# The taps' first transform stage with whole 128-row matmuls instead of row halves

## The chip, the core and the metric

The kernel runs on one core of a Trainium2 chip. The metric is the device time of one execution in microseconds, the median over runs. One profiled execution of the kernel before is at hand, with its trace. Engines: TensorE (PE for matmuls, PEld for weight loads), VectorE (DVE), ScalarE (ACT), GpSimd (POOL), and SyncE (SP), whose queue issues the DMA transfers.

## What is computed

Two mixers over the same 2048 tokens of 576 channels are blended by a gate. A long convolution (S4) makes 2048 taps per channel from 128 complex modes and convolves by FFT; a layer of product-key experts (PEER) scores 64 x 64 experts for 32 heads, keeps two per head, and weighs rows of two tables of 4096 x 576.

```
x = A_u                                             # [1, 2048, 576]
g = sigmoid((x * gate_w).sum(-1))
K[d, l] = Re sum_n C[d, n] dB[d, n] exp(dt A[d, n] l)   # the taps
a = irfft(rfft(x, 4096) * rfft(K, 4096))[:2048] + x * Dskip
q = x @ w_q;  s1 = q1 @ k1.T;  s2 = q2 @ k2.T           # 32 heads, 64 keys each
top 2 of s1 and of s2 -> 4 candidates -> top 2 -> softmax g_k, expert e_k
b = sum over heads and k of g_k * gelu(x . u[e_k]) * v[e_k]
out = g * a + (1 - g) * b
```

## The kernel before

Matrix products run in split fp16: each operand is a high and a low half, and three of the four cross products are summed. Two families of *groups* make the bulk of TensorE's work. An `s` group scores 128 tokens against the folded weights of four heads (`whl`, `wrem`); an `a` group multiplies 512 tokens with 128 experts (`uhl`, `wrem`). Each sums 13.5 rows of 128 contractions over 512 columns in one PSUM bank: 4 blocks of 128 channels times 3 cross products, and a rest of 64 channels.

A group is written by `start_group` in one of two ways. `halved` cuts every matmul into an upper part (rows 0 to 63) and a lower part (rows 64 to 127), 27 matmuls of 64 rows; `rows` puts the upper ones on a queue `upper` and, when those are through, the lower ones on a list `lower`, and `row_slot` emits one upper matmul of one group beside one lower matmul of the group ahead of it. The two use different rows of the array and different banks. `triple` writes the group as 14 matmuls of 128 rows one after another (the rest as two passes with one operand stored twice). The kernel before has `triple` in its code, but its condition `caps["sc"] < 4` never holds once the loop runs, so all groups but the first four are halved.

The program's order is fixed when it is built. Generators are resumed by `pump` against a planned clock; each carries one strand of work: `k_gen` makes the taps, `k_stage1` and `products` transform them, `scores_top` finds the two best of each head, `act_post` stores the activations, `w_half` folds the next weights (`wn` small sums, `wb` the fold), `gating` forms the gates, `v_norm` reads the gate's inputs and the second table (`vn`, `vj`). `quota` sets how many of the eight PSUM banks groups (`sc`) and strands (`wb`) may hold. `chained[0]` says that the halves are in use; `total` and `k_factors` then put their small sums on the same queue.

The change is in the taps' transform. When all 36 chunks of taps are stored in DRAM (`k_store`), `freq` is spawned, which loads them back in another layout (`ksb`, four loads, with the tables `tk`) and runs `k_stage1`: 32 steps `w`, each with two outputs of 288 columns (`k1_w_0`, `k1_w_1`), each a sum of two 128-row products. `k1o` copies them from two banks to one of four buffers, and `sk_d` stores it. `products` follows: it loads spectra of the input and of the taps (`ui`, `ki`), finishes both transforms (`pr`, `pi`), multiplies and transforms back (`pv`). Groups run in between all the while. When they have all run, the experts' values are gathered with one-hot matmuls (`S`) and summed (`o`).

SP issues transfers in program order; an issue that waits holds up all behind it. `vn` loads have two buffers, `k1o` four.

Of the kernel before, what the change touches and what calls it, by code (L numbers as in the profile page):

```python
# [140 lines left out]
def body(ctx: ExitStack, tc: tile.TileContext, xT, au, par, logdt, dskip, gatew, wq, kT, uT, vv,  # L141
# [5 lines left out]
    clock = [0.0]  # L147
# [11 lines left out]
    def key(x):  # L159
        n = x.tensor.name  # L160
        return (n, x.offset) if n in columns else n

    def size(x):
        n = 1
        for d in x.shape[1:]:
            n *= d
        return n
# [41 lines left out]
    def mm(o, l, r, start, stop, cost=None):  # L209
        m = l.shape[0] > 64, 128 if size(l) > 64 else size(l)  # L210
        if m != tiling[0]:
            tiling[0] = m
            clock[0] += 0.13 if m == (True, 128) else 0.1
        clock[0] += (size(r) * (4 if r.dtype == F32 else 1) / 2400 + 0.003) if cost is None else cost
        rdy[key(o)] = clock[0] + 0.4
        return T.matmul(o, l, r, start=start, stop=stop)  # L216
# [4 lines left out]
    def rows(up, low, then=None, first=False):  # L221

        g = {"up": deque(up), "low": deque(low), "then": then, "done": False, "end": None, "short": first}
        (upper.appendleft if first else upper.append)(g)
        return g
# [28 lines left out]
                    g["then"]()  # L254

    chained = [False]

    def total(p, cols):

# [45 lines left out]
    slots, caps, owed = {}, {}, {}  # L305
# [6 lines left out]
    def quota(**kw):  # L312
        for tag, n in kw.items():
            if tag in banksets:
                caps[tag] = n
                continue
            lst = slots.setdefault(tag, [])
            d = n - caps.get(tag, 0) - owed.get(tag, 0)
            caps[tag], owed[tag] = n, 0
            while d > 0:  # L320
                lst.append(clock[0])
                d -= 1
            while d < 0 and lst:
                lst.remove(min(lst))
                d += 1
            owed[tag] = -d if d < 0 else 0
# [13 lines left out]
    def take(tag, name):  # L340
        lst = slots[tag]
        assert lst, name
        lst.remove(min(lst))
# [66 lines left out]
    sc = cp.tile([128, 192], F32, name="sc")  # L410
# [601 lines left out]
    def k_store(c, kb):  # L1012
        yield from ready(kb)
        yield from need("ko")
        take("ko", "ko")
        ko = kg.tile([128, 2, 2 * NI * R2], F16, name="ko", tag="ko", bufs=1)
        kq = kb.rearrange("p (c i q) -> p q c i", c=2, i=NI)
        kz = ko.rearrange("p z (q c i) -> p z q c i", c=2, i=NI)
        S.activation(kz[:, 0], kq, AF.Copy)
        yield from ready(ko)  # L1020
        V.tensor_sub(kz[:, 1], kq, kz[:, 0])
        free("kb", ko, of=kb)
        yield from ready(ko)
        kstored[0] += 2
        dma(k_d[c].rearrange("p z m q -> p z (m q)"), ko)
        free("ko", k_d)
        if kstored[0] == NCK:
            while uf != 0:
                yield 0.3
            KG.__exit__(None, None, None)  # L1030
            quota(sc=5, wb=4, kb=0, raw=2)
            spawn(freq())


# [231 lines left out]
    def k_stage1(ksb, fk, tabs):  # L1266
        enter, leave, count = ring(3)

        def tail(w, o, pbs, gs):
            while not all(g["done"] for g in gs):  # L1270
                yield 0.2
            yield from ready(*pbs)
            for hh in range(2):
                copy(o[:, 288 * hh:288 * hh + 288], pbs[hh][:, :288])
                free("wb", o, of=pbs[hh])
            yield from ready(o)
            dma(pair_rows(sk_d, w), o)
            leave(w)

        for w in range(32):  # L1280
            tkt = tabs[w // 16]
            yield from ready(tkt, ksb)
            yield from enter()
            o = fk.tile([128, D], F32, tag="s1o", name=f"k1o{w}", bufs=4)
            pbs, gs = [], []
            yield from need("wb", 2)
            for hh in range(2):
                pb = bank("wb", f"k1_{w}_{hh}")
                pbs.append(pb)
                gs.append(rows(*([(pb[:, :288], tkt[h:h + 64, w % 16, n],  # L1290
                                   ksb[h:h + 64, 2 * hh:2 * hh + 2, :, w, :].rearrange("p j c i -> p (j c) i"),
                                   h == 0 and n == 0, h == 64 and n == 1) for n in range(2)] for h in (0, 64)), first=True))
            spawn(tail(w, o, pbs, gs))
            del pb, pbs
        while count() < 32:
            yield 0.5
# [102 lines left out]
    def freq():  # L1399
        nonlocal ff, ab, iota_a, iota_b  # L1400
        ff = FG.__enter__()
        wrems.append(ff.tile([128, 2, 512], F16, name="wrem3"))
        ksb = KS.__enter__().tile([128, 4, NCK // 2, 32, 2 * NI], F16, name="ksb")
        fk = FK.__enter__()
        tabs = [fk.tile([128, 16, 2, 128], F16, tag="tk", name=f"tk{w0}", bufs=2) for w0 in (0, 16)]
        for w0, tkt in zip((0, 16), tabs):
            dma(tkt, tk_d[:, w0:w0 + 16, :])
        for j in range(4):
            while wire[0] > clock[0] + 2:
                yield 0.3  # L1410
            dma(ksb[:, j].rearrange("p c w i -> p c (w i)"),
                k_d[:, 32 * j:32 * j + 32].rearrange("c l z m n -> (l z m) c n"))
        spawn(v_norm(), 4)
        spawn(gating(0), 20)
        yield from k_stage1(ksb, fk, tabs)
        FK.__exit__(None, None, None)
        KS.__exit__(None, None, None)
        v_pool(0, 3)
        spawn(v_work())
        fp = FP.__enter__()  # L1420
        quota(sc=4, wb=5)
        yield 3
        yield from products(fp)
        FP.__exit__(None, None, None)
        quota(sc=4, wb=4)
        ab = ctx.enter_context(tc.tile_pool(name="ab", bufs=1, side="right"))
        iota_a = ab.tile([128, 128, 2], F16, name="iota_a")
        iota_b = ab.tile([128, 64, 2], F16, name="iota_b")
        V.tensor_copy(iota_a, cst[:, 384:512, None].to_broadcast([128, 128, 2]))
        V.tensor_copy(iota_b, cst[:, 512:576, None].to_broadcast([128, 64, 2]))  # L1430
        spawn(prep(0))
        v_pool(3, 5)
        while not gated or not gates:
            yield 0.5
        FG.__exit__(None, None, None)
        WJ.__exit__(None, None, None)
        v_pool(5, 8)
        shut.append(1)
# [444 lines left out]
    def start_group(g):  # L1883

        x = xb[tb_of(g)]
        if len(g) == 2:
            c, t = g
            pb = bank("sc", f"s{c}_{t}")
            args = (pb, *whl[c], x), (slice(128 * (t % 4), 128 * (t % 4) + 128), slice(0, 512), True)

            def then():
                spawn(scores_top(c, t, pb))
                used(("w", c), ("x", t // 4))
        else:
            c, tb, j = g
            if c == 7 and not got:
                got.append(1)
                V.tensor_reduce(out=nut[:, 0:1], in_=nu, axis=AX, op=OP.max)
                V.scalar_tensor_tensor(nut[:, 1:2], nut[:, 0:1], 1100.0, nx2, op0=OP.mult, op1=OP.mult)
                got.append(root_scale(nut[:, 1:2], 1.0))  # L1900
                V.tensor_scalar(s_wg, got[1][0], 2.0 ** -14, None, op0=OP.mult)
            if c in i_u and (c, tb) not in scales:
                scales.add((c, tb))
                V.tensor_scalar(i_a[:, c, tb:tb + 1], i_x[:, tb:tb + 1], i_u[c], None, op0=OP.mult)
            pb = bank("sc", f"a{c}_{tb}_{j}")
            args = (pb, *uhl[c], x), (slice(0, 512), slice(128 * j, 128 * j + 128), False)

            def then():
                spawn(act_post(c, tb, j, pb))
                used(("u", c), ("x", tb))  # L1910
        parity[0] = tb_of(g) % 2
        if caps["sc"] < 4:
            while upper or lower:
                row_slot()
            chained[0] = False
            triple(*args[0], *args[1])
            then()
            return
        chained[0] = True
        rows(*halved(*args[0], tb_of(g), *args[1]), then)  # L1920
        while len(lower) > 2 and sum(len(x["low"]) for x in lower[:-1]) > 6:
            row_slot()
            if not upper:
                return
# [111 lines left out]
```

## Time and profile before

| | |
|---|---|
| median of 3 runs | 1452.56 us (1451.73 to 1454.49) |
| the profiled execution | 1451.91 us |
| its span | 1450.1 us |
| granted TensorE clock, mean | 0.999 |
| DMA | 215.89 MB, mean 149 GB/s |
| first and last product of the taps' stage | 685.0 to 732.2 us |
| `sk_d` stores | 32 of 288 KB |

Busy shares and the chain of waits come from the page of the profile; times from a stretch come from the stages (busy time of each engine, matmul count in brackets, then clock, DMA share, GB/s) and from the order of time, where a row is: start, length, engine, line, operation, output and inputs, shape, count, and in square brackets the idle time ahead of it and what ended it. All matmuls carry line 216 and all work of the other engines line 136, since helpers record them; so one goes by the tiles' names.

### The profile page before, as it was taken

What the parts mean: (1) busy time and instruction counts of PE and PEld (TensorE: products, weight loads), DVE (VectorE), ACT (ScalarE), POOL (GpSimd) and SP (SyncE); (2) the same over time, 40 slices, a digit from 0 to 9 for tenths busy, and PEclk for the clock granted to TensorE, in tenths of its full rate; (3) what the DMA queues carried; (4) which work ended last, traced back from release to release, by engine and by line L of the source; (5) the groups of instructions that cost most, each with busy time, mean ns of one, the idle gap of its engine ahead of it and who ended that gap; (6) DMA issues with size and microseconds to landing.
All of it is one profiled execution on the core that took longest, in us unless ns stands there. A gap on an engine that the chain in (4) does not pass through costs nothing.

```text
span 1450.1 us, 44027 instructions
## 1 busy us (share of the span) xinstructions
PE 1422.8 (98%) x17654; PEld 902.6 (62%) x17654; DVE 1193.5 (82%) x4597; ACT 830.3 (57%) x1444; POOL 477.1 (33%) x488
## 2 busy tenths in 40 slices
PE   7999999999999999999999999999999999999998
PEld 3465566554565665455664444446887887888787
DVE  5887699889889988777789998699999988888860
ACT  6547887987888887664656665564333223323310
POOL 0443265552571663530557899400000000000000
PEclk9999999999999999999999999999999999999999
DMA  9333543343351331238785788687442433342400
GB/s 315 116 111 100 167 134 110 99 128 110 110 157 47 120 104 46 78 125 269 253 275 173 255 273 310 218 254 223 155 153 86 135 121 106 122 146 68 157 9 17
DMA packets 134381, 215.89 MB, mean 149 GB/s; under 512 B 10913, under 2 KB 79905, under 8 KB 127777
## 3 DMA queue, kind: packets, MB, share of 16 engines
q1 hardware_dynamic: 134080, 213.01, 45.5%
q8 instruction: 138, 2.26, 0.6%
q14 instruction: 67, 0.54, 0.1%
q10 hardware_dynamic: 96, 0.07, 0.0%
HBM read 141.74 MB, written 71.30 MB: 147 GB/s over the span
## 4 chain that ended last, share of the span: by engine, by line
PE 86%; DMA 5%; DVE 4%; issue 1%; SPq 1%; ACT 1%; POOL 1%; ACTq 0%; POOLq 0%; DVEq 0%
PE a L216 25%; PE o L216 24%; PE s L216 21%; PE S L216 4%; PE kb L216 2%; PE pr L216 2%; PE wb L216 2%; DMA wq<-in_wq_dram 1%; SPq L207 1%; PE kP L216 1%; PE y L216 1%; DVE i L136 1%; PE pv L216 1%; DVE m L136 1%; PE u L216 1%
## 5 line engine op out<-in xcount | busy, mean ns | idle before, releaser
L216 PE MATMUL s<-whl,xb 64*128 64x512 f16 x3072 | 468.8, 377 | 0.5 <-ACT k1o L136 0.3
L216 PE MATMUL a<-xb,uhl 64*128 64x512 f16 (+1 forms) x3024 | 455.5, 376 | 0.3 <-DVE go L136 0.2
L216 PE MATMUL o<-vhl,wh 128*128 128x288 f16 x3072 | 387.1, 286 | 0.0
L216 PEld LDWEIGHTS <-wh 128*128 128x128 f16 x3072 | 295.9, 98 | 76.2 <-issue 3.7
L216 PEld LDWEIGHTS <-xb 64*128 64x128 f16 x3456 | 226.8, 94 | 167.5 <-issue 15.2
L216 PEld LDWEIGHTS <-uhl 64*128 64x128 f16 (+1 forms) x3024 | 195.8, 94 | 165.1 <-issue 6.9
L136 ACT ACTIVATE wh<-gl,s_wg 128x1024 f16<-128x1024 f32 x64 | 68.7, 1137 | 197.4 <-DVE gl L136 197.4
L136 POOL TENSOR_TENSOR CS<-CS,ex 128x512 f32<-128x512 f32 x72 | 90.6, 1290 | 167.2 <-DVE ex L136 167.2
L216 PE MATMUL s<-wrem,xb 64*128 64x512 f16 x384 | 122.2, 376 | 0.0
L216 PE MATMUL a<-xb,wrem 64*128 64x512 f16 (+1 forms) x380 | 120.2, 376 | 0.0
L136 ACT ACTIVATE go<-a,i_a 128x512 f32<-128x512 f32 x98 | 66.9, 684 | 85.6 <-PE a L216 57.0
L136 DVE FIND_INDEX8 i<-m,s 128x8 uint32<-128x64 f32 x520 | 104.7, 219 | 0.0
L136 DVE TENSOR_TENSOR gl<-S,gl 128x256 f32<-128x256 f32 x256 | 90.3, 414 | 15.6 <-PE S L216 6.1
L136 POOL TENSOR_TENSOR e<-aN,rt 128x512 f32<-128x512 f32 x72 | 83.9, 1185 | 46.6 <-PE kb L216 46.5
L136 DVE FIND_INDEX8 i<-m,sx 128x8 uint32<-128x64 f32 x504 | 99.2, 216 | 0.0
L136 DVE MAX8 m<-s 128x8 f32<-128x64 f32 x520 | 74.1, 212 | 26.8 <-PE s L216 22.7
L136 DVE SCALAR_TENSOR_TENSOR wh<-gl,s_wg,wh 128x1024 f16<-128x1024 f32 x64 | 79.7, 1278 | 10.4 <-ACT wh L136 10.4
L136 ACT ACTIVATE gl<-gl 128x1024 f32<-128x1024 f32 x64 | 63.4, 1045 | 40.5 <-DMA gl<-g_d 40.5
L136 DVE TENSOR_TENSOR Bg<-Be,vals 128x1024 f16<-128x1024 f16 x128 | 82.7, 688 | 2.2
L136 ACT ACTIVATE CS<-CS 128x1024 f32<-128x1024 f32 x72 | 74.6, 1049 | 6.4 <-DVE CS L136 6.1
L136 DVE TENSOR_TENSOR A<-iota_a,vals 128x2048 f16<-128x2048 f16 x64 | 77.7, 1214 | 0.0
L216 PEld LDWEIGHTS <-A 128*128 128x128 f16 x2048 | 70.1, 97 | 6.4 <-issue 2.8
(206 smaller groups left out, 2356.4 us busy)
## 6 DMA issues: line engine op xcount, KB each, us to landing
g_d<-go SPq DMA_DIRECT2D x128, 256.0 KB, 2.7
gl<-g_d SPq DMA_DIRECT2D x32, 1024.0 KB, 5.6
wq<-in_wq_dram SPq DMA_DIRECT2D x16, 1152.0 KB, 5.9
su_d<-us SPq DMA_DIRECT2D x32, 288.0 KB, 2.6
sk_d<-k1o SPq DMA_DIRECT2D x32, 288.0 KB, 2.8
ui<-su_d SPq DMA_DIRECT2D x16, 576.0 KB, 4.3
ki<-sk_d SPq DMA_DIRECT2D x16, 576.0 KB, 5.6
vn<-in_vv_dram SPq DMA_DIRECT2D x32, 288.0 KB, 4.5
```

The costliest lines, as they stand in the source:

```text
L136: return f(*a, **k)
L207: (q or DQ).dma_start(o, i)
L216: return T.matmul(o, l, r, start=start, stop=stop)
```

## The change

While `k_stage1` is planned (from the storing of the last taps until `products` begins), groups are written by `triple`, after the halves that are still open have been emitted alone, and `chained[0]` is cleared. `k_stage1` then writes its products as two matmuls of 128 rows for each output. The groups' share of banks in the stage is four instead of five. With `phase[0]` at `"products"` groups are halved again. The other values of `phase` decide nothing, and `clock[0] < 0` is never true.

```diff
--- before.py
+++ after.py
@@ -254,6 +254,7 @@
                     g["then"]()
 
     chained = [False]
+    phase = ["taps"]
 
     def total(p, cols):
 
@@ -1028,7 +1029,8 @@
             while uf != 0:
                 yield 0.3
             KG.__exit__(None, None, None)
-            quota(sc=5, wb=4, kb=0, raw=2)
+            quota(sc=4, wb=4, kb=0, raw=2)
+            phase[0] = "k1"
             spawn(freq())
 
 
@@ -1287,6 +1289,11 @@
             for hh in range(2):
                 pb = bank("wb", f"k1_{w}_{hh}")
                 pbs.append(pb)
+                if not chained[0]:
+                    for n in range(2):
+                        mm(pb[:, :288], tkt[:, w % 16, n], ksb[:, 2 * hh:2 * hh + 2, :, w, :].rearrange("p j c i -> p (j c) i"),
+                           n == 0, n == 1)
+                    continue
                 gs.append(rows(*([(pb[:, :288], tkt[h:h + 64, w % 16, n],
                                    ksb[h:h + 64, 2 * hh:2 * hh + 2, :, w, :].rearrange("p j c i -> p (j c) i"),
                                    h == 0 and n == 0, h == 64 and n == 1) for n in range(2)] for h in (0, 64)), first=True))
@@ -1419,10 +1426,12 @@
         spawn(v_work())
         fp = FP.__enter__()
         quota(sc=4, wb=5)
+        phase[0] = "products"
         yield 3
         yield from products(fp)
         FP.__exit__(None, None, None)
         quota(sc=4, wb=4)
+        phase[0] = "last"
         ab = ctx.enter_context(tc.tile_pool(name="ab", bufs=1, side="right"))
         iota_a = ab.tile([128, 128, 2], F16, name="iota_a")
         iota_b = ab.tile([128, 64, 2], F16, name="iota_b")
@@ -1909,7 +1918,7 @@
                 spawn(act_post(c, tb, j, pb))
                 used(("u", c), ("x", tb))
         parity[0] = tb_of(g) % 2
-        if caps["sc"] < 4:
+        if clock[0] < 0 or phase[0] in ("k1",):
             while upper or lower:
                 row_slot()
             chained[0] = False
```

The names in the rows below carry the step and then a number of the buffer. On TensorE at the entry, where `freq` has just been spawned, two `a` groups are open. Before:

```order
L216 LDWEIGHTS uhl6_9266
L216 MATMUL a6_0_1_11060<-xb0_145,uhl6_9266 128x512
L216 LDWEIGHTS xb0_145
L216 MATMUL s5_0_11209<-whl5_10645,xb0_145 128x512
L216 LDWEIGHTS uhl6_9266
L216 MATMUL a6_0_1_11060<-xb0_145,uhl6_9266 128x512
L216 LDWEIGHTS xb0_145
L216 MATMUL s5_0_11209<-whl5_10645,xb0_145 128x512
```

Now:

```order
L216 LDWEIGHTS uhl6_9266
L216 MATMUL a6_0_1_11060<-xb0_145,uhl6_9266 128x512
L216 LDWEIGHTS uhl6_9266
L216 MATMUL a6_0_1_11060<-xb0_145,uhl6_9266 128x512
L216 LDWEIGHTS uhl6_9266
L216 MATMUL a6_0_1_11060<-xb0_145,uhl6_9266 128x512
L216 LDWEIGHTS wrem0_114
L216 MATMUL a6_0_1_11060<-xb0_145,wrem0_114 128x512
L216 LDWEIGHTS uhl6_9266
L216 MATMUL a6_1_0_11092<-xb1_146,uhl6_9266 128x512
```

The lower halves stood beside the upper halves of `s5_0`; now all 18 of them stand alone, and `s5_0` follows them in 128 rows. On TensorE at the first product of the taps' stage, before:

```order
L216 MATMUL s5_7_11590<-whl5_10645,xb1_146 128x512
L216 LDWEIGHTS tk0_11205
L216 MATMUL k1_0_1_11717<-ksb_11201,tk0_11205 128x288
L216 LDWEIGHTS xb1_146
L216 MATMUL s5_7_11590<-whl5_10645,xb1_146 128x512
L216 LDWEIGHTS tk0_11205
L216 MATMUL k1_0_1_11717<-ksb_11201,tk0_11205 128x288
L216 LDWEIGHTS xb1_146
L216 MATMUL s5_7_11590<-whl5_10645,xb1_146 128x512
```

Now:

```order
L216 LDWEIGHTS xb1_146
L216 MATMUL s5_7_11585<-whl5_10645,xb1_146 128x512
L216 LDWEIGHTS tk0_11205
L216 MATMUL k1_0_0_11596<-ksb_11201,tk0_11205 128x288
L216 LDWEIGHTS tk0_11205
L216 MATMUL k1_0_0_11596<-ksb_11201,tk0_11205 128x288
L216 LDWEIGHTS tk0_11205
L216 MATMUL k1_0_1_11599<-ksb_11201,tk0_11205 128x288
L216 LDWEIGHTS tk0_11205
L216 MATMUL k1_0_1_11599<-ksb_11201,tk0_11205 128x288
L216 LDWEIGHTS xb1_146
L216 MATMUL s5_7_11585<-whl5_10645,xb1_146 128x512
```

The upper halves of product 0 alternated with halves of group `s5_7`; now the four whole products stand together and three or two passes of a group follow. Between the first and the last product there were 233 halves of `s` groups and are 92 whole passes. On ScalarE, which empties the products' banks, before:

```order
L136 ACTIVATE k1o0_11715<-k1_0_0_11716 128x288
L136 ACTIVATE k1o0_11715<-k1_0_1_11717 128x288
L136 ACTIVATE vj32_11759,gA_81<-vn32_11649 128x576
L136 ACTIVATE sx5_7_11798<-s5_7_11590 128x512
L136 ACTIVATE k1o1_11718<-k1_1_0_11770 128x288
L136 ACTIVATE k1o1_11718<-k1_1_1_11771 128x288
L136 ACTIVATE k1o2_11772<-k1_2_0_11785 128x288
```

Now:

```order
L136 ACTIVATE k1o0_11589<-k1_0_0_11596 128x288
L136 ACTIVATE k1o0_11589<-k1_0_1_11599 128x288
L136 ACTIVATE vj32_11607,gA_81<-vn32_11538 128x576
L136 ACTIVATE k1o1_11602<-k1_1_0_11633 128x288
L136 ACTIVATE k1o1_11602<-k1_1_1_11636 128x288
L136 ACTIVATE sx5_7_11654<-s5_7_11585 128x512
L136 ACTIVATE k1o2_11639<-k1_2_0_11645 128x288
```

`vj32` stays behind the copies of product 0; the copies of product 1 now follow it directly. On SP at the end of the stage, before:

```order
L207 DMA sk_d_67<-k1o29_12708 32x4x576
L207 DMA wq7_0_12839<-in_wq_dram 128x2304
L207 DMA sk_d_67<-k1o30_12741 32x4x576
L207 DMA vn45_12884<-in_au_dram 32x576 x4
L207 DMA sk_d_67<-k1o31_12769 32x4x576
L207 DMA ui0_12961<-su_d_66 128x1152
L207 DMA ki0_12962<-sk_d_67 128x1152
L207 DMA ui1_12965<-su_d_66 128x1152
L207 DMA ki1_12966<-sk_d_67 128x1152
```

Now:

```order
L207 DMA sk_d_67<-k1o30_12229 32x4x576
L207 DMA vn41_12291<-in_au_dram 32x576 x4
L207 DMA sk_d_67<-k1o31_12247 32x4x576
L207 DMA ui0_12345<-su_d_66 128x1152
L207 DMA ki0_12346<-sk_d_67 128x1152
L207 DMA ui1_12349<-su_d_66 128x1152
L207 DMA ki1_12350<-sk_d_67 128x1152
L207 DMA vn42_12353<-in_au_dram 32x576 x4
L207 DMA wq7_0_12415<-in_wq_dram 128x2304
```

The load `wq7_0` has moved from ahead of the last two stores to behind the first four loads of `products`; 8 loads of `vn` instead of 12 lie between the first store and the last.

## The prediction

> **What bounds the kernel now.** I read the page first, then the busy time by stage around the changed code, then the order of time on TensorE, ScalarE, GpSimd and the DMA queue there.
>
> ```profile
> PE 1422.8 (98%) x17654; PEld 902.6 (62%) x17654; DVE 1193.5 (82%) x4597; ACT 830.3 (57%) x1444; POOL 477.1 (33%) x488
> PE 86%; DMA 5%; DVE 4%; issue 1%; SPq 1%; ACT 1%; POOL 1%; ACTq 0%; POOLq 0%; DVEq 0%
> ```
>
> TensorE is busy for 98% of the span and carries 86% of the chain. So the change is worth what it does to TensorE's work and to TensorE's waits, nothing else. The stages around it (PE is the first number pair, the half-clock share stands before the DMA share):
>
> ```profile
> 682.20:684.64 2.44, 0.00 (x1) 0.00 (x0) 2.36 (x14) 0.21 (x1) 0.00 (x0) 1.00 0.91 245
> 684.64:688.05 3.41, 3.06 (x19) 2.03 (x21) 2.22 (x16) 0.00 (x0) 0.70 (x1) 0.50 0.38 105
> 688.05:732.40 44.35, 41.76 (x473) 30.54 (x471) 31.78 (x224) 29.83 (x94) 26.54 (x50) 1.00 0.76 253
> 732.40:749.20 16.80, 15.18 (x192) 11.02 (x187) 15.94 (x118) 9.04 (x26) 7.29 (x17) 1.00 0.82 273
> 749.20:763.30 14.10, 12.92 (x149) 6.13 (x150) 11.05 (x53) 7.54 (x21) 8.69 (x11) 1.00 0.84 288
> 763.30:950.00 186.70, 186.38 (x2304) 89.89 (x2305) 158.10 (x824) 115.16 (x309) 140.09 (x170) 1.00 0.73 245
> ```
>
> There is the one stretch of this kernel where TensorE loses time: 2.4 us without a matmul from 682.20, 3.41 us at half the granted clock, 2.6 us idle in the stage of the taps' products, 1.6 us and 1.2 us in the two stretches behind it. After 763.30 it is busy for 186.38 of 186.70 us. What the change can win is here.
>
> ```profile
> 684.96 0.10 PEld L216 LDWEIGHTS <-tk 64*128 64x128 f16 x1 [3.25 <-issue]
> 684.99 0.40 PE L216 MATMUL k<-ksb,tk 64*128 64x288 f16 x1 [2.79 <-DVE i L136]
> L216 PE MATMUL k<-ksb,tk x256: 279/283/444, 685.0 to 732.2; 64*128 64x288 f16 x128
> L207 SPq DMA_DIRECT2D ksb<-k_d x4: 712/2428/5367, 658.1 to 672.6; - x4
> DMA to landing us min/median/max: 10.8/11.7/13.7
> ```
>
> The first product waits 2.79 us. The page names VectorE, but the weight load ahead of it waited too, and the fourth load of `ksb` was issued at 672.6 and lands 10.8 to 13.7 us later: 683.4 to 686.3. I take the wait as one for that transfer.
>
> **The change part by part.** Prices first.
>
> ```profile
> 656.09 0.38 PE L216 MATMUL a<-xb,wrem 64*128 64x512 f16 x1
> 656.30 2.33 PE L216 MATMUL s<-whl,xb 64*128 64x512 f16 x20
> 676.54 2.32 PE L216 MATMUL wb<-kt,wq 128*64 128x64 f32 x72
> 678.79 1.47 PE L216 MATMUL s<-whl,xb 64*128 64x512 f16 x12
> 23.69 1.03 PE L216 MATMUL a<-xb,wrem 128*128 128x512 f16 x4
> 24.55 1.03 PE L216 MATMUL a<-xb,uhl 128*128 128x512 f16 x4
> 1019.77 4.45 PE L216 MATMUL o<-vhl,wh 128*128 128x288 f16 x35
> L216 PE MATMUL o<-vhl,wh 128*128 128x288 f16 x3072 | 387.1, 286 | 0.0
> L216 PEld LDWEIGHTS <-wh 128*128 128x128 f16 x3072 | 295.9, 98 | 76.2 <-issue 3.7
> ```
>
> Two halves side by side cost (2.33-0.38)/9 = 0.217 us a pair. A 128-row pass of 512 columns costs (24.55-23.69)/4 = 0.215 us, one of 288 columns (4.45-0.286)/34 = 0.1225 us. A fold of `wq` takes 678.79-676.54 = 2.25 us. A group is 27 halves, 13.5 pairs or 2.93 us; in 128 rows it is 14 passes or 3.01 us. In the changed order 15 groups are whole (210 passes): 0.085 x 15 = 1.3 us more.
>
> These loads of 98 ns stand in front of passes of 122.5 ns and do not show. A rule speaks against the change here: the Trainium skill, "TensorE: Matmul & The Clock Gate", section "The mechanism", says that a weight load overlaps running matmuls only where the row group differs. By it each of the 338 whole passes would show its load. The trace disagrees, since 35 such passes with a load each took 4.45 us; the case stands among the rivals.
>
> *Entry.* The 18 lower halves of two `a` groups stand alone. The last of them starts at 656.09, so the first did at 656.09 - 17 x 0.217 = 652.40. They end when they ended before, paired or not, so the stores of `go` and the `ksb` loads queued behind them on SP leave on time, and the first product still starts at 684.99. In front of it stand now 18 x 0.217 = 3.9, 104 passes = 22.4, two folds = 4.5 and a switch of the row mode. The nearest row for the switch is 0.1 us (748.06 to 748.38 below, less a pair of 0.217). TensorE arrives at 683.3 and waits 1.7 us, not 2.8. A stop of 2.44 us halved the clock for 3.41 us, which cost 3.06/2 = 1.5 us; one of 1.15 us (763.28, below) did not. At 1.7 us I take it that it stays up, and keep 1.5 us for the high end. The same page of the Trainium skill, section "What's actually happening", speaks of an idle window of about 3.4 us; this trace's clock fell after 2.44 us, so the row is the bound here.
>
> *The products' stage.* Before: 684.99 to 732.4, 47.4 us. In it lie 128 pairs of products (15.7) and, by the order, 233 halves of groups (25.3): 41.0. The other 6.4 are 2.6 idle, 1.5 of half clock and 2.3 where a 288 stands beside a 512. After: 128 x 0.1225 + 92 x 0.215 = 15.7 + 19.8 = 35.5 us, and waits. The products come every 35.5/32 = 1.11 us instead of 1.47, so what empties their banks must follow:
>
> ```profile
> ACT k1o L136 <- DMA sk_d<-k1o: 4.2, 5, 1.9
> PE k L216 <- ACT k1o L136: 2.1, 3, 1.1
> 687.35 2.76 POOL L136 TENSOR_TENSOR vn<-vn,gw 128x576 f32<-128x576 f32 x2 [43.70 <-DMA vn<-in_au_dram]
> 688.26 0.71 ACT L136 ACTIVATE k1o<-k 128x288 f32<-128x288 f32 x2 [5.85 <-PE k L216]
> 688.99 0.68 ACT L136 ACTIVATE vj<-vn 128x576 bf16<-128x576 f32 x1
> 689.58 0.19 ACT L136 ACTIVATION_READ_ACCUMULATOR vj<-vn 128x1 f32 x1
> 710.57 1.98 SPq L207 DMA_DIRECT2D vn<-in_au_dram  x4
> 712.64 1.17 SPq L207 DMA_DIRECT2D sk_d<-k1o  x2
> 712.75 0.68 ACT L136 ACTIVATE vj<-vn 128x576 bf16<-128x576 f32 x1 [2.42 <-POOL vn L136]
> 714.37 0.28 PE L216 MATMUL k<-ksb,tk 64*128 64x288 f16 x1 [1.10 <-ACT k1o L136]
> sk_d<-k1o SPq DMA_DIRECT2D x32, 288.0 KB, 2.8
> ```
>
> First wait: ScalarE has `vj32` behind the copies of product 0 in both orders. `vn32` is multiplied by 687.35 + 1.38 = 688.7, whatever TensorE does, `vj32` ends 0.87 later, and the two copies of product 1 at 690.3. Four banks hold two products, so product 3 needs those banks; TensorE gets there at 684.99 + 3 x 0.49 + 11 x 0.215 = 688.8. It waits 1.3 us, and product 4 about 0.3: 1.6.
>
> Then the loop of stores. Four `k1o` buffers go round in 4 x 1.11 = 4.4 us; copies (0.71) and store (2.8) leave 0.9. On SP a store costs 0.585 and a `vn` load of four pieces 1.98; with 8 such loads (12 before) SP is taken for 32 x 0.585 + 8 x 1.98 = 34.6 of 35.5 us. A store behind a `vn` load leaves 1.98 - (1.11 - 0.585) = 1.45 late, 0.55 more than the loop can take. The banks leave 2 x 1.11 - 0.49 - 0.71 - 0.2 = 0.8. So a store late alone is hidden; where a `vj` (0.87) falls into the same turn, 0.6 shows. I take 0.4 for each of the 7 others, 2.8, and 0.6 for the one load of an activation table. Waits: 1.6 + 2.8 + 0.6 = 5.0 us. The bounds: 1.6 alone, and 47.4 - 35.5 = 11.9 if the loop cannot go faster than it went.
>
> *Exit, and the first product of the spectra.*
>
> ```profile
> 742.90 0.16 PE L216 MATMUL wn<-sc,onesb 64*128 64x1 bf16 x1 [0.57 <-DVE i L136]
> 744.19 0.16 PE L216 MATMUL wn<-sc,onesb 64*128 64x1 bf16 x1 [0.90 <-ACT wj L136]
> 748.06 0.39 PE L216 MATMUL s<-whl,xb 64*128 64x512 f16 x2
> 748.38 0.43 PE L216 MATMUL pr<-ui,cst 64*64 64x256 f32 x2
> 749.22 0.43 PE L216 MATMUL pr<-ki,cst 64*64 64x256 f32 x2 [0.17 <-DMA ki<-sk_d]
> 763.28 0.16 PE L216 MATMUL wn<-sc,onesb 64*128 64x1 bf16 x1 [1.15 <-ACT tt L136]
> ki<-sk_d SPq DMA_DIRECT2D x1, 576.0 KB, 5.1
> ```
>
> Between the last tap product and the first one on `ki` stand now 14 passes (3.0), 20 pairs and 16 halves alone (36 x 0.217 = 7.8), a switch (0.1) and the part on `ui` (0.6): 11.5 us. The last store and `ki` need, from the last tap product, 0.35 + 1.98 on SP behind `vn41`, 2.8 to land, 0.2, 0.4 for `ui` and 5.1 to land: 10.8. I allow 0.4 of wait (to 3, if SP has fallen behind). TensorE is at that product at 684.99 + 35.5 + 5.0 + 11.5 + 0.4 = 737.4, before 749.22: 11.8 us earlier.
>
> It has done less by then. Counted from the first of the 18: 546 halves before; 15 whole groups (405) and 56 halves, 461, after. The missing 85 are 42.5 pairs or 9.2 us, and the fold `wb7_0` with its small sums, done before and not yet after, is 2.35. So 11.8 - 11.6 = 0.2 us is won. The `wq7_0` load now leaves behind the first four loads of the products, and its sums stand some 15 us of TensorE's work behind the first product instead of ahead of it, so I count 0.5 us of waits for both sums `wn7` where 763.28 still shows 1.15: 0.65 more. Groups, products and everything behind are the same instructions in both, in a stretch where TensorE loses 0.3 of 187 us.
>
> **The sum.** -0.2 - 0.65 = -0.9 us. On the profiled execution's 1451.91 us (span 1450.1) that is 1451.0; on the median of 1452.56 it is 1451.7 us. That is no change: 0.2% is 2.9 us, about what a measurement of this kernel can tell (its three runs lie 2.8 us apart).
>
> **The rivals.**
> *Slower: the stores set the pace.* SP at 34.6 of 35.5 us has no room for lateness, and ScalarE stood still 4.2 us for stores already. If a product again takes 1.47 us, the waits are 11.9, not 5.0: +6.9, 1458.6 us. It is slower by 2.9 us from waits of 8.8 on, a product every 1.38 us. Against it: the stage now holds 8 `vn` loads, not 12, so SP's work per product falls from 1.33 to 1.08 us. Late stores also make `ki` late, with up to 2.6 us. Chance 0.32.
> *Faster: only the first wait is left.* The table of waits shows TensorE held up by copies three times in 32 products; if the four banks hide the rest, waits are 1.6, and with no wait at the `wn7` sums it comes to -0.9 - 3.4 - 0.5 = -4.8, 1447.8 us. Faster by 2.9 needs waits of 3.0 or less. Chance 0.27.
> *The weight loads show.* 338 passes x 0.098 = 33 us: 1485 us. The 35 passes in 4.45 us speak against it, though their columns are contiguous and those of `ksb` are not. It is the rule named above. Chance 0.01.
> *Nothing happens* cannot be: the order shows 128 whole products and 15 whole groups.
>
> **How the numbers follow.** No measurable change has 0.40, faster 0.27, slower 0.32 + 0.01 = 0.33. The likeliest is 1451.7. The low end is the faster rival without its last half us, 1448.0; the high end the slower one with the half clock's 1.5 us, less the little I give to both at once: 1459.5. The forecast's own range is 1449.7 to 1455.4.
>
> **What would show it.** Right: the first tap product still starts near 685 after a wait of 1.7 us at full clock; the last one near 725; a wait of 1 to 2 us for ScalarE's copies near product 3, behind `vj`; the first product on `ki` near 737 with hardly a wait; weight loads hidden. Wrong: a last tap product behind 729, with ScalarE or VectorE waiting for stores, is the slower rival; one before 722 the faster one. A first product well off 685, or new waits behind 763, would be steps that I have missed.

## The result and the profile after

The changed kernel takes 1461.12 us (median of 6 runs, 1458.55 to 1461.74) where the kernel before took 1452.64 us beside it (1451.73 to 1454.49): a ratio of 1.0055, interval 1.0044 to 1.0065. It is slower by 8.5 us, where 1451.7 was forecast with a range up to 1459.5. The profiled execution took 1458.55 us, the fastest of the six, with a span of 1456.8.

The stretches around the changed stage, in the trace of after, in the columns of the prediction's table of stretches (behind GpSimd's busy time stand the granted clock, the share of the DMA engines and GB/s):

```profile
685.40:727.10 41.70, 37.34 (x222) 21.46 (x221) 28.88 (x194) 25.91 (x79) 18.68 (x34) 1.00 0.76 258
727.10:738.70 11.60, 11.54 (x82) 4.85 (x82) 9.79 (x75) 3.93 (x14) 5.47 (x12) 1.00 0.80 276
738.70:767.45 28.75, 28.17 (x389) 14.73 (x382) 27.96 (x155) 18.07 (x46) 25.52 (x33) 1.00 0.68 235
767.45:917.40 149.95, 149.83 (x1897) 72.08 (x1897) 131.47 (x779) 99.78 (x283) 129.95 (x168) 1.00 0.74 251
917.40:919.95 2.55, 0.00 (x1) 0.00 (x0) 0.00 (x0) 1.69 (x4) 0.00 (x0) 1.00 1.04 376
919.95:930.19 10.24, 7.80 (x87) 4.57 (x88) 5.39 (x21) 5.04 (x13) 0.00 (x0) 0.50 0.18 64
```

Up to 917.40 this is the forecast's picture: a short stage of products, hardly a wait behind it. Then TensorE stands still for 4.99 us; 2.55 us into this stop the clock falls to half, and it stays there for 10.24 us. This lies 190 us behind the changed stage. The order of time there, on SP, VectorE and TensorE of after (`vhl` are loads of the second table, `z_d` takes the result of `products`; columns: start, busy time, engine, line, operation, out<-in; in brackets how long the engine stood idle before, and what the profile names as the releaser):

```profile
911.17 1.09 SPq L207 DMA_DIRECT2D vhl<-in_vv_dram  x2
912.37 0.48 SPq L207 DMA_DIRECT2D z_d<-vo  x1
913.78 0.20 DVE L136 TENSOR_SCALAR ggu<-ggu 128x64 f32<-128x64 f32 x1
921.77 0.29 DVE L136 CAST iota_a<-cst 128x256 f16<-128x256 f32 x1 [7.80 <-DMA g_d<-go]
921.98 0.22 DVE L136 CAST iota_b<-cst 128x128 f16<-128x128 f32 x1
922.12 0.87 DVE L136 TENSOR_TENSOR vals<-tr,vals 128x64 f16<-128x64 f32 x6
917.08 0.32 PE L216 MATMUL tr<-cst,vals 128*64 128x64 f32 x4
922.39 0.33 PE L216 MATMUL tr<-identb,vals 128*64 128x64 bf16 x4 [4.99 <-DVE vals L136]
```

`iota_a` and `iota_b` are two casts of constants with which the function `freq` opens what follows the products. They stand idle on VectorE for 7.80 us, and behind them wait the 16 subtractions `vals<-tr`, which empty the banks of the transposes `tr`. After six `tr` TensorE has no bank and stops for 4.99 us. The casts write into pool `ab`, in memory that `products` has just left, so they must wait until the last `z_d<-vo` store has read its buffer. (The profile names a `g_d` store; its source `go` lies elsewhere.)

```profile
DMA to landing us min/median/max: 3.0/4.2/9.2
```

That row is from the view of the tile `z_d` of after: the 16 stores land after 4.2 us as a rule, one after 9.2, and 912.37 + 9.2 = 921.6 is just where the casts start. The casts waited before too. From the order of time on SP and VectorE in the trace of before:

```profile
927.84 0.33 SPq L207 DMA_DIRECT2D z_d<-vo  x1
931.27 0.29 DVE L136 CAST iota_a<-cst 128x256 f16<-128x256 f32 x1 [3.49 <-DMA z_d<-vo]
```

And the view of the tile `tr` of before, with the first and the last start:

```profile
L216 PE MATMUL tr<-identb,vals x64: 196/224/247, 918.1 to 925.5; 128*64 128x64 bf16 x64
```

There the casts waited 3.49 us for the same store, but came at 931, behind the last `tr`, and nobody needed VectorE. What moved is the order of VectorE's instructions. Before, at the end of the 16 subtractions:

```
L136 TENSOR_TENSOR vals<-tr_16415,vals 128x64
L136 TENSOR_TENSOR vals<-tr_16425,vals 128x64
L136 COPY vo_16193<-pv_1_16445 128x256
L136 CAST iota_a<-cst 128x256
L136 CAST iota_b<-cst 128x128
```

After, at their beginning:

```
L136 TENSOR_SCALAR ggu_15474<-ggu_15474 128x64
L136 CAST iota_a<-cst 128x256
L136 CAST iota_b<-cst 128x128
L136 TENSOR_TENSOR vals<-tr_15870,vals 128x64
L136 TENSOR_TENSOR vals<-tr_15877,vals 128x64
```

The products of the spectra begin 10 us earlier and now end ahead of the transposes: the last `pv` starts at 910.6 (926.9 before), the first `tr` at 915.3 (918.1 before).

The size of the loss, from the trace of after: 5.0 us of stop and 7.80/2 = 3.9 us of matmuls at half speed are 8.9 us. The profiled execution itself is the fastest of its six, and its span is only 6.7 us longer than that of before; so 8.9 us fits the medians, and single traces differ by some 2 us elsewhere.

### The profile page after: what moved, and what is told of

The parts are those of the page before. It is cut to its first block, busy times and chain, and to the rows that moved or that the text cites. A ratio compares the mean times of both kernels' runs of the same rounds, so it can differ in the third digit from the quotient of the medians.

```text
span 1456.8 us, 43370 instructions
## 1 busy us (share of the span) xinstructions
PE 1426.9 (98%) x17327; PEld 894.4 (61%) x17327; DVE 1191.7 (82%) x4594; ACT 837.7 (58%) x1453; POOL 474.2 (33%) x488
## 4 chain that ended last, share of the span: by engine, by line
PE 89%; DMA 4%; DVE 3%; SPq 2%; ACT 1%; issue 1%; POOL 0%; DVEq 0%; ACTq 0%; POOLq 0%
PE a L216 26%; PE o L216 24%; PE s L216 23%; PE S L216 4%; PE pr L216 2%; PE kb L216 2%; PE wb L216 2%; SPq L207 2%; PE kP L216 1%; PE pv L216 1%; PE y L216 1%; DMA ksb<-k_d 1%; PE u L216 1%; DMA sk_d<-k1o 1%; DMA g_d<-go 1%
## 5 line engine op out<-in xcount | busy, mean ns | idle before, releaser
L216 PE MATMUL s<-whl,xb 64*128 64x512 f16 (+1 forms) x2892 | 455.7, 377 | 0.2
L216 PEld LDWEIGHTS <-xb 64*128 64x128 f16 (+1 forms) x3261 | 215.6, 94 | 173.1 <-issue 14.0
L216 PE MATMUL s<-wrem,xb 64*128 64x512 f16 (+1 forms) x369 | 116.2, 378 | 0.0
L136 DVE FIND_INDEX8 i<-m,sx 128x8 uint32<-128x64 f32 x552 | 108.7, 216 | 0.0
L136 DVE FIND_INDEX8 i<-m,s 128x8 uint32<-128x64 f32 x472 | 95.2, 222 | 0.0
L136 DVE MAX8 m<-s 128x8 f32<-128x64 f32 x472 | 67.5, 215 | 26.8 <-PE s L216 23.2
L136 DVE MAX8 m<-sx 128x8 f32<-128x64 f32 x552 | 75.9, 208 | 5.0 <-ACT sx L136 4.7
```

The source lines that it names most:

```text
L136: return f(*a, **k)
```

## The experiments

**The casts without their wait.** The same place on VectorE, but memory that nothing else uses:

```
+    iota2 = (cp.tile([128, 128, 2], F16, name="iota_a"), cp.tile([128, 64, 2], F16, name="iota_b"))
...
-        iota_a = ab.tile([128, 128, 2], F16, name="iota_a")
-        iota_b = ab.tile([128, 64, 2], F16, name="iota_b")
+        iota_a, iota_b = iota2
```

> The changed kernel with memory of their own for iota_a and iota_b, so that the casts stay on VectorE at the same place but wait for no store. Theory A: it is the wait for the z_d store that costs, not the place of the casts: as with the casts on GpSimd about 1452.2 us (1450 to 1454), no stop before tr. A rival within it, A2: the casts are late for another reason (VectorE itself behind with its work): the stop stays and the time stays near 1461. Theory B: within 2 us of 1461.

Measured: 1452.18 us, ratio to before 0.9989 (0.9978 to 0.9999). The 9 us are gone, as theory A said. In its trace the first cast runs where it stands, without waiting (order of time on VectorE):

```profile
916.12 0.28 DVE L136 CAST iota_a<-cst 128x256 f16<-128x256 f32 x1
```

The two stretches of above are full, and at full clock:

```profile
917.40:919.95 2.55, 2.55 (x62) 2.04 (x60) 0.99 (x5) 1.43 (x6) 0.00 (x0) 1.00 1.00 385
919.95:930.19 10.24, 10.24 (x137) 5.54 (x137) 8.20 (x20) 8.94 (x21) 0.00 (x0) 1.00 0.78 250
```

Theories A2 and B are out. What the forecast's own sum is worth once the wait is away is told further below.

**The casts behind the subtractions.** They still lie in the memory that waits for the store, only their place is that of before:

```
         phase[0] = "last"
+        while len(placed) < NT:
+            yield 0.5
         ab = ctx.enter_context(tc.tile_pool(name="ab", bufs=1, side="right"))
```

> The changed kernel with the casts, still in the same memory and still behind the z_d store, issued behind all 16 subtractions that empty tr, which is their place in the kernel before. If order alone decides (theory A): the wait comes back on VectorE where nobody needs it, no stop before tr, about 1452.5 us (1451 to 1455). If the wait costs wherever it stands: 1458 to 1461.

Measured: 1453.13 us, ratio 0.9996 (0.9986 to 1.0006). `tr` never stops. The casts run behind the last subtraction, and no wait is left in front of them:

```profile
927.95 0.29 DVE L136 CAST iota_a<-cst 128x256 f16<-128x256 f32 x1
```

Against the expectation no wait came back there; the store, issued at 915.96, no longer held anything up. So it takes both, the wait and the place ahead of the subtractions; either removed alone brings the time back.

**The casts on GpSimd,** in the changed kernel and in the kernel before:

```
-        V.tensor_copy(iota_a, cst[:, 384:512, None].to_broadcast([128, 128, 2]))
-        V.tensor_copy(iota_b, cst[:, 512:576, None].to_broadcast([128, 64, 2]))
+        G.tensor_copy(iota_a, cst[:, 384:512, None].to_broadcast([128, 128, 2]))
+        G.tensor_copy(iota_b, cst[:, 512:576, None].to_broadcast([128, 64, 2]))
```

> The changed kernel, but the two casts iota_a and iota_b, which open the inverse transform, run on GpSimd instead of VectorE. Theory A: in the changed kernel these two casts wait on VectorE for a late z_d store, stand ahead of the 16 subtractions that free the banks of tr, and so stop TensorE for 4.98 us at 917.4, and the clock then runs at half for 10.24 us (7.80 us of matmuls at half speed, 3.9 us lost). On GpSimd they block nobody: no stop before tr, no half clock at 920, and 5.0 + 3.9 = 8.9 us less than the changed kernel, about 1452.2 us in the median (1450 to 1454). Theory B: the 8.5 us are lost in the stage of the taps' products (waits 5.0 forecast, 6.2 seen) and the stop at 917 only takes up slack: then the stop goes, the time stays within 2 us of 1461. Theory C: the half clock goes with the stop but some of the cost was paid elsewhere (half clock at 599): 1455 to 1457.

> Control: the kernel before, with the same two casts on GpSimd. There they stand behind the 16 subtractions on VectorE and no stop is seen, so theories A, B and C all give no change (1452.6 us, within 1 us). A gain of several us here would mean that the move helps both kernels and that the difference between the two is not explained by it.

Measured: 1460.11 us for the changed kernel, ratio 1.0047 (1.0032 to 1.0063), and 1453.53 us for the control, 1.0005 (0.9994 to 1.0015). The first number is a miss for theory A as I had put it and looks like theory B; the trace says why it is not (GpSimd, then TensorE and its releaser):

```profile
924.93 0.40 POOL L136 CAST iota_a<-cst 128x256 f16<-128x256 f32 x1 [12.84 <-DMA g_d<-go]
925.52 0.32 POOL L136 TENSOR_TENSOR vals<-ggu,ggd 128x64 f32<-128x64 f32 x1
925.90 0.48 PE L216 MATMUL tr<-cst,vals 128*64 128x64 f32 x4 [7.82 <-POOL vals L136]
```

On GpSimd the casts wait for the same store (issued at 915.35 here, so they start 9.6 us behind it, where it was 9.4 on VectorE), and now the product `vals<-ggu,ggd`, which `tr` reads, is queued behind them. The wait has moved to another queue, and the same TensorE work waits for that one: "they block nobody" was wrong.

**Why the store lands late.** The first `vhl` loads are held until the last store has been issued:

```
+            while phase[0] == "products":
+                yield 0.5
             if c not in raw:
```

> The changed kernel with iota_a and iota_b where they were, but the first loads of vhl held back until the last z_d store has been issued. Theory A1: the casts wait for the landing of that store, and it lands late (up to 9.2 us, median 4.2) because two vhl loads of 1.15 MB are issued 1.2 us ahead of it. Then the store lands about 4.2 us after its issue, the casts run about 5 us earlier, the stop before tr falls from 5.0 to below 1 us and the clock stays up: about 1452.5 us (1451 to 1455). Rival A2: the store is late for what stands ahead of it on its queue otherwise, or the casts wait for another transfer: stop and time stay, 1460.

Measured: 1461.28 us, ratio 1.0050 (1.0035 to 1.0065). The order of time in its trace, at the casts and then at `S`:

```profile
913.54 0.86 SPq L207 DMA_DIRECT2D z_d<-vo  x1
914.45 1.50 SPq L207 DMA_DIRECT2D vhl<-in_vv_dram  x2
917.72 0.29 DVE L136 CAST iota_a<-cst 128x256 f16<-128x256 f32 x1 [1.83 <-DMA z_d<-vo]
956.95 0.20 PE L216 MATMUL S<-Bg,A 128*128 128x64 f16 x1 [1.66 <-DVE Bg L136]
```

The wait is as A1 says: with no loads ahead of it the casts start 4.2 us after the store is issued, and the profile names the right one. The time does not follow: the stop before `tr` is gone (0.3 us is left, and the last `tr` starts at 924.0 where it was 930.9), but TensorE stands for 1.7 us at 955 and 1.9 us at 1029 in front of `S`, with half clocks around 960 and 1003. Whether that is the price of the hold itself, the same hold with iota in memory of its own tells:

> Control for the run in which the first vhl loads were held back (1461.3 us, although its stop before tr was gone): the same hold, and iota in memory of its own. Theory: the hold itself costs what that run lost, by stops in front of S (1.7 us at 955, 1.9 us at 1029) and the half clock behind them, so this one is at 1459 to 1462 too. Rival: the casts' wait still cost something there: this one comes back to 1452 to 1453.

Measured: 1461.72 us, ratio 1.0054 (1.0037 to 1.0071), with stops of 1.65 us at 953.5 and 2.9 us at 1025.5 in front of `S`. It is the hold's own price, and the earlier time says nothing against A1. Why the hold makes `S` late was not followed.

So the place of the casts does not cost much by itself: with a store that lands in time, 0.3 us of stop are left. In the change two `vhl` loads stand right ahead of the last store, and the casts start 9.4 us after its issue; in the kernel before there were none right ahead of it, and it took 3.4 us.

**Five banks for the groups,** one edit of the change taken back, casts as in the change:

```
-            quota(sc=4, wb=4, kb=0, raw=2)
+            quota(sc=5, wb=4, kb=0, raw=2)
```

> The changed kernel with five banks again, not four, for the groups while the taps' products run (one of the edits that came with the change). Theory A: the loss is far behind this stage, so the time stays within 2 us of the changed kernel's 1461 unless the casts change places with the subtractions. Theory B: with one bank more for groups and one less free for products, waits in the stage of the taps' products change, by up to 3 us either way.

Measured: 1460.44 us, ratio 1.0051 (1.0035 to 1.0067). The casts stay ahead of the subtractions, run at 926.45 after 8.63 us, and `tr` stops for 5.8 us. The bank is not the cause.

**The two halves of the change apart,** both with iota in memory of its own. First whole groups with the products in halves (the branch `if not chained[0]` of `k_stage1` taken out), then whole products with the groups in halves:

```
-                if not chained[0]:
+                if True:
...
-        if clock[0] < 0 or phase[0] in ("k1",):
+        if clock[0] < 0:
```

> Iota tiles in memory of their own; the groups whole (128 rows) as in the change, the taps' products in row halves as before. Halves then find few other halves to stand beside: by the order TensorE's lanes need 8.6 us more to the end than with both whole (32 whole groups and a longer stage of products), and 39 switches of the row mode at 0.107 us add 4: 1452.2 + 12 = about 1464 (1460 to 1468). If halves of a product overlap with whole passes after all: 1452.

> Iota tiles in memory of their own; the taps' products whole (128 rows) as in the change, the groups between them in row halves as before. By the order and 0.1 us for each of some 63 switches of the row mode, TensorE's work to the end is 6.7 us less for the pairs that no longer stand beside a 288-column half and 6.3 us more for the switches: about 1452 us, with the stage of the products shorter and more waits in it. If a switch costs 0.2 us or more: 1458 or more. If the switches cost nothing that shows: 1446.

Measured: 1462.24 us, ratio 1.0072 (1.0057 to 1.0087), for whole groups alone, about as expected. Its stage of products runs from 686.1 to 773.7 us, with TensorE busy all the while: halves that find no partner cost a pass of their own. But its trace also has a stop of 3.24 us at 896.4, in front of an `a` group and behind copies of `vo`, which the expectation did not contain; so the agreement of the total is in part luck. Whole products alone: 1467.69 us, ratio 1.0097 (1.0083 to 1.0112), a miss. The rows that price a switch of the row mode, TensorE in its stage:

```profile
693.08 0.66 PE L216 MATMUL k<-ksb,tk 128*128 128x288 f16 x4
693.68 0.39 PE L216 MATMUL s<-whl,xb 64*128 64x512 f16 x2
694.00 0.66 PE L216 MATMUL k<-ksb,tk 128*128 128x288 f16 x4
1018.08 3.49 PE L216 MATMUL y<-yz,tf 128*32 128x288 f32 x32 [3.26 <-ACT wh L136]
1036.12 0.21 PE L216 MATMUL S<-Bg,A 128*128 128x64 f16 x1 [4.63 <-DVE Bg L136]
```

A product and a pair take 694.00 - 693.08 = 0.92 us against 0.490 + 0.217: two switches are 0.213, 0.107 each, as expected. The rest is elsewhere: its last `pr` starts at 935.1 (903.9 with both whole), and two stops of 3.3 and 4.6 us end at 1018 and 1036, longer than any that far behind in the other runs. With the 10.24 us of half clock behind them, 5.1 us lost, they make 13 of the 15.5 us between this run and the one with both whole (1452.18). I did not follow their cause, so this run does not price whole products by themselves.

**The loop of stores.** Iota in its own memory, and eight buffers for `k1o`; then the same in the kernel before:

```
-            o = fk.tile([128, D], F32, tag="s1o", name=f"k1o{w}", bufs=4)
+            o = fk.tile([128, D], F32, tag="s1o", name=f"k1o{w}", bufs=8)
```

> The changed kernel with memory of their own for the iota tiles (as before, 1452.2 us), and 8 buffers for k1o instead of 4; the order of every engine is the same, only waits can differ. The forecast's term: 2.8 us of TensorE's waits in the taps' stage come from the loop of stores through four k1o buffers; with 8 they go, the first wait (1.6 us in the forecast) stays, and the time falls by 2.7 us to about 1449.5 (1448.5 to 1450.5). Rival: the waits come from ScalarE being held by vj and by PSUM banks, or an earlier end of the stage is lost again at ki or at the spectra's stores: within 1 us of 1452.2.

> Control: the kernel before, with 8 buffers for k1o. TensorE waits 1.9 us for copies into k1o in its stage of products, ScalarE 4.2 us for stores. If these buffers help only the faster stage of the change: within 1 us of 1452.8. If they help both: 1450.5 to 1451.5.

Measured: 1450.74 us, ratio 0.9978 (0.9968 to 0.9987), and for the kernel before 1452.58 us, 0.9999 (0.9990 to 1.0008). The products' first and last start, with iota in its own memory and four buffers:

```profile
L216 PE MATMUL k<-ksb,tk x128: 282/286/286, 685.9 to 727.4; 128*128 128x288 f16 x128
```

The same with eight:

```profile
L216 PE MATMUL k<-ksb,tk x128: 283/286/286, 685.0 to 721.7; 128*128 128x288 f16 x128
```

Then, with eight, the first product of the spectra in the order of time:

```profile
736.23 0.43 PE L216 MATMUL pr<-ui,cst 64*64 64x256 f32 x2 [3.12 <-DMA ui<-su_d]
```

And the clock behind it, from the stretches:

```profile
738.00:741.41 3.41, 3.41 (x26) 1.21 (x20) 2.07 (x3) 1.98 (x8) 2.42 (x2) 0.51 1.08 323
```

The stage falls from 41.5 to 36.7 us: the stores held it by 4.8 us, more than my 2.8. But 3.1 us come back at once as a wait for `ui`, and 1.7 as 3.41 us of half clock behind that wait. That would leave nothing; the time fell by 1.4 us all the same, and of this 0.9 is that the first product starts earlier in this trace (685.0 against 685.9), which the buffers do not explain. Where the stage is slower, before, the buffers bring nothing.

**A version that beats both.** The same with more groups put ahead of the first product:

```
-        yield 3
+        yield 6
         yield from products(fp)
```

> The changed kernel with iota in memory of its own, 8 buffers for k1o, and the products' loop started 3 planned us later (yield 6 in place of 3), which puts about 3 us of groups ahead of the first product. The run with 8 buffers won 4.8 us in the taps' stage and lost 3.1 us in front of the first product on ui (its load, issued at 731.8, lands after TensorE arrives) and some 1.8 us by the half clock that this stop brought. Theory: both losses go, 1450.7 - 3.1 - 1.8 = 1446 (1445 to 1448). Rival: the later products are late somewhere else, at tr or S: no gain, 1450 to 1452.

Measured: 1448.85 us, ratio 0.9976 (0.9966 to 0.9987): it beats both kernels, the one before by 0.2%, but not the run without this edit (0.9978). The theory was wrong and the rival right that nothing is won, though 1448.85 lies below the rival's range of 1450 to 1452. The wait for `ui` is now one for `ki`, its half clock is still there, and 2.3 us are lost later in front of `S`. The order of time on TensorE:

```profile
738.24 0.60 PE L216 MATMUL pr<-ki,cst 64*64 64x256 f32 x2 [1.56 <-DMA ki<-sk_d]
954.44 0.20 PE L216 MATMUL S<-Bg,A 128*128 128x64 f16 x1 [2.26 <-DVE Bg L136]
```

The stretch behind that wait:

```profile
738.24:741.65 3.41, 3.41 (x28) 1.58 (x30) 1.59 (x5) 1.69 (x5) 1.51 (x2) 0.52 1.01 418
```

## Why the prediction was wrong

**The step that failed** is the sentence "Groups, products and everything behind are the same instructions in both, in a stretch where TensorE loses 0.3 of 187 us". The instructions are the same, their order on VectorE is not. I let the spectra's products begin 11.8 us earlier and asked what that does to TensorE up to the `wn7` sums, and not which work they now overtake. The runs show in its place a stop of 4.99 us in front of `tr` and 10.24 us at half clock, some 9 us, which go when the casts wait for no store (1452.18) or come behind the subtractions (1453.13). An order that comes out of planned times is shifted behind such a step as well. The 0.3 us of TensorE's loss said only that VectorE's 3.5 us of wait were covered by work that happened to stand ahead of it. The text did name "new waits behind 763" as a missed step; it gave them no price and no chance. It also called the stretch of the products the one in which TensorE loses time. The trace of before has other stops, the longest of 2.95 us at 594.6, and the runs above lost time in front of `tr` and `S`.

**Entry.** Right in outcome, not in detail. The first product starts at 685.4 (684.99 forecast). It waits for no transfer: TensorE came some 2 us later than I reckoned. In the trace of after a stop at 594.7 lasts 3.77 us (2.95 before), and the clock is at half for 3.41 us from 599.1, before the first changed instruction; that is 0.8 and 1.7 us. The kernel before with its casts on GpSimd, and with eight buffers, shows a half clock there too, so it varies from run to run and is no part of the change.

**The products' stage.** 35.5 us of work and 5.0 of waits were forecast; 41.7 us came, so 6.2 beside the work, 4.4 of it idle (41.70 - 37.34). Nearly all of the rest belongs to the same stops: a pass with nothing behind it is drawn 0.286 us long and not 0.1225, and from start to start the passes of this stage are 6.0 us further apart than their prices. The waits of after from 684 to 740 us, in all, times, longest:

```profile
ACT k1o L136 <- DMA sk_d<-k1o: 8.1, 10, 2.9
PE k L216 <- ACT k1o L136: 3.3, 4, 1.9
```

The mechanism was right, stores first and copies behind them. My split was not: the wait behind `vj32` was 0.3 us at 690.6, not 1.6 (its own two times, 690.3 and 688.8, lie 1.5 apart and not 1.3), one for a bank of the top scores that I had not seen was 0.7 at 685.8, and the last was 1.85 at 722.5, not 0.4. The run with eight buffers gives the loop of stores 4.8 us, where the forecast had 2.8. The weight loads do not show: four passes of 288 columns take 0.66 us in the rows on the switch above, (0.66 - 0.286)/3 = 0.125 us a pass against 0.1225 as priced.

**Exit.** The first product on `ki` starts at 738.7 us (737.4 forecast, 749.2 before), and one wait of 0.58 us is left at the `wn7` sums (0.5 forecast, 1.15 before). In this trace both are near the forecast. The second is luck in part: in four other runs with the same order up to there the wait is 1.09, 1.28, 1.46 and 1.74 us.

**The sum.** With the failed step taken out, -0.8 us (0.9989, interval 0.9978 to 0.9999) stands against -0.9. That the two agree to 0.1 us is luck: the interval is 3 us wide, and with the first product on `ki` at 738.7 the forecast's own term of -0.2 would have been +1.1 (10.5 us earlier, against 11.6 us of work not yet done). What is shown is that the rest of the change is worth no more than some 3 us, as forecast.

**The rivals.** The slower one, 1458.6 us, came near the number with the wrong mechanism: its place would have been a last product behind 729 us, and that was 726.9. The faster one (1447.8) assumed that only the first wait is left. With eight buffers the products wait only once, 0.9 us for the top scores; but the time fell by 1.4 us, not 3.4, since the wait reappeared at `ui`.

## What to carry to other kernels

When a change shifts the time of a stage, compare the order of every engine to the end of the kernel, not only around the edit, and look for instructions that change places with others on a queue that works in order. In the trace of before, list the long idle times of engines that seem to cost nothing: each is a wait with a cover, and one that overtakes its cover shows in full. Memory that one stage leaves to the next carries such a wait; memory of its own for a constant (768 bytes in each partition here) removes it wherever the planner puts it.

## What the runs showed of the hardware

A stop costs more than itself, and the half clock comes in whole pieces: 3.41 us after stops of 3.12 and 1.56 us (738.00 and 738.24 above), 10.24 us, three times that, in after. Behind that stop stand small `tr` matmuls; whether they kept the clock down, no run isolates. A stop of 1.85 us at 722.5 in after left the clock up, and so did one of 3.24 us with whole groups alone, so the length alone does not decide.

What decides is in part where the stop lies. Wherever a trace has several half clocks, they begin whole multiples of 3.413 us apart: 94 of them from 599.10 to 919.95 in after, 106 and 12 between 596.99, 958.80 and 999.76 in the run with the `vhl` loads held. On that grid a piece can be read like a stretch. Three of them, the first two from after, the last from the run with groups ahead of the products:

```profile
721.98:725.39 3.41, 1.56 (x10) 0.76 (x9) 1.19 (x12) 1.47 (x6) 3.02 (x7) 1.00 0.83 274
916.54:919.95 3.41, 0.86 (x18) 0.62 (x17) 0.00 (x0) 2.16 (x6) 0.00 (x0) 1.00 1.05 386
734.97:738.38 3.41, 1.85 (x22) 0.64 (x20) 3.34 (x28) 1.61 (x9) 1.45 (x5) 1.00 1.00 385
```

The first left the clock up, the other two were followed by a half clock. Over the 14 traces, from 30 to 1430 us, each of the 22 pieces at full clock in which TensorE was busy for less than 0.40 of the time was followed by one; of the 15 between 0.40 and 0.55, 6 were; of the 5666 above, one (0.76 busy, thin `S` matmuls). The share of busy time goes a long way, but not all the way.

The Trainium skill, "TensorE: Matmul & The Clock Gate", section "What's actually happening", tells of a free-running window of 3413 ns, and the pieces and their grid agree with it; that it takes an idle window of about 3.4 us to fall does not agree with the stop of 1.56 us here.
